# A linear-attention and feed-forward kernel: the hand-written TensorE order replaced, with later landings assumed for two kinds of transposing DMA

## The chip, the cores and the metric

The kernel runs on one core of a Trainium2 chip. The metric is the device time of one execution in microseconds (us); lower is better. The core has TensorE (PE in the profile, and PEld for its weight loads), VectorE (DVE), ScalarE (ACT), GpSimd (POOL) and SyncE (SP). SP does no arithmetic here. It issues nearly all DMAs, in the order of its own queue.

## The reference

```python
xn = layernorm(x)                          # x: 2048 x 448, bfloat16
q, k, v = split(xn @ wqkv)                 # 16 heads of 28
phi_q = concat(softmax(q @ w_phi), softmax(-(q @ w_phi)))   # per head, 28 + 28
phi_k = concat(softmax(k @ w_phi), softmax(-(k @ w_phi)))
kv = einsum("hsf,hsd->hfd", phi_k, v);  z = sum_s phi_k
o  = (phi_q @ kv) / (phi_q @ z + 1e-6)
out = x + o @ wo + silu(xn @ w1) @ w2      # w1: 448 x 1792, w2: 1792 x 448
```

## The kernel before

The 2048 tokens are 16 tiles of 128. The kernel records every operation with the buffers that it reads and writes, puts all of them in order with a list scheduler of its own (`schedule`), and emits one queue for each engine with the waits that the recorded dependences need. The scheduler's costs are figures written in the source. A DMA gets a time to issue, a transfer and a latency (`o.lat`).

For TensorE the order of most of the program is written out by hand, in the string `PLAN` (lines 334 to 342). Each word is one piece of work, and `strict` ties each TensorE operation to the one before it. The scheduler fits the other engines' queues to that order. The words are:

- `aF3@4`, `bF3`: first and second half of a feed-forward block, 256 columns of the hidden layer for 512 tokens, in PSUM banks 4 and 5. There are 28 blocks, seven for each 512 tokens. Blocks 0, 1 and 2 stand ahead of the plan. `av`, `ak` and `aq` with their `b` halves are the v, k and q projections of two tiles. The halves are matmuls on 64 rows of the array, two at a time: six in the first half, eight in the second. The second half waits until the first is finished (`o.after`).
- `f0@2`: one of four folds of w_phi into the q and k weights. Each takes two banks and needs all nine transposed weight loads `wT_dma0` to `wT_dma8`. ScalarE copies two reference columns out (`fold_ref`), and VectorE then takes them from the rest (`fold_sub`, line 636). Only after the third `fold_sub` of a fold are its banks free.
- `K0-6`: the sum over tokens phi_k x v for tiles 0 to 5. `M`: that sum is masked for use. `s4`: phi_q of tiles 4 and 5 is normalised on GpSimd and then transposed by a DMA named `phqT` (the first six in the order one tile at a time, the rest two at a time).
- `U4@2`: attention of tile 4 in bank 2. VectorE then divides by the denominator (`den`, `rden`, `o`), and a DMA named `oT_dma` transposes the result. `W4`: three matmuls with wo on that transposed tile. `R4,7`: the remaining rows of wo for tiles 4 and 7, as 64-row matmuls, and then the addition and the output's DMA. `F4@0:14` and `Y1:9`: the second feed-forward matmul, 14 or 9 of its 14 steps. `E15`: the end of the last tile, in two halves of 224 columns.

A word without `@` goes to the bank that the same tile or block already has. A `U` without one goes to bank 7.

The order of the DMAs on SP follows from the scheduler too. A `phqT` or `oT_dma` waits at the head of that queue until its data are there, and everything behind it waits as well. All `phqT` and `oT_dma` are issued by `dma_t` (line 583).

Of the kernel before, what the change touches and what calls it, by code (L numbers as in the profile page):

```python
# [8 lines left out]
ACTF = mybir.ActivationFunctionType  # L9
# [131 lines left out]
class _Prog:  # L141
# [76 lines left out]
    def schedule(self):  # L218
# [55 lines left out]
        while done < n:  # L274
# [56 lines left out]
TAIL = {"act": 110.0, "dve": 85.0, "pool": 45.0}  # L331
SIGNAL = {("act", "pe"): 60.0, ("act", "dve"): 40.0, ("dve", "pe"): 100.0, ("dve", "sp"): 30.0, ("dve", "dve"): 34.0,
          ("pool", "pe"): 100.0}
PLAN = """aF3@4 bF3 aF4@0 aF6@2 av2@6 bF4 bF6 aF5@4 av0@0 bv0 bF5 aF12@2 bv2 aF11@0 aF13@4 bF12 bF11 bF13 aF10@6 aF8@0 f0@2 f3@4
bF8 bF10 f2@2 aF9@0 f1@4 aF7@6 bF9 bF7 ak2@4 bk2 av12@6 av10@0 ak14@2 bv12 bk14 bv10 ak4@4 av14@6 bk4 ak0@2 bv14 av6@0
bk0 bv6 Y2@6:5 Y2:6 Y2:3 ak6@2 ak8@0 bk6 av8@4 av4@6 bv8 bk8 bv4 ak10@4 ak12@2 bk10 aq4@0 bk12 K0-2 bq4 aq6@4 K2-6 bq6
aq8@2 s4 aq0@0 bq8 K6-8 bq0 aF17@4 K8-10 bF17 aF14@2 aF19@0 bF14 bF19 aF16@4 aF23@2 K10-16 bF16 aF27@0 M bF23 bF27
aF24@5 aF20@2 bF24 aF26@0 bF20 aF15@4 bF26 s6 bF15 aF21@6 aF22@2 bF21 aF18@4 s8 bF22 s0 aF25@0 aq2@6 bF18 bF25 bq2
aq12@2 aq10@4 bq12 bq10 F9@1:2 F9:4 F9:8 U7 F7@6:10 s2 F7:4 Y1@5:2 Y0@0:6 U4@2 Y0:8 s10 U0@4 Y1:9 U9 Y1:3 F4@0:1 F4:13
U2 W4 U6@3 U3@5 W7 W9 s12 W0@2 R4,7 aq14@3 R0,9 bq14 Y3@5:2 Y3:3 U5@2 U1 F5@6:5 F5:9 U8@2 F6@0:11 F6:3 Y3:5 U13@2 U11  # L340
F11@4:14 Y3:2 U10@3 s14 W2@2 W5 W6 U12 F14@3:6 F10@1:7 U14 Y3:2 F10:7 F14:6 W10 F13@7:10 F14:2 W11 W14 R6,14 R5,10 R2,11
F13:4 F8@5:8 F8:4 F8:2 W3@6 W8 W13 F12@1:2 F12:1 F12:11 U15@0 W12 W1@4 R1,8,13 R12,3 F15@23:6 F15:8 E15"""


def bass_parallel_sum__linear_kernel_hedgehog__dense_activation_silu__prompt_kernel(
# [36 lines left out]
    with es:  # L382
        def sb(name, shape, dt):
            return es.enter_context(nc.sbuf_tensor(name, shape, dt))
# [46 lines left out]
        ones_bf = sb("ones_bf", [128, 128], BF16)  # L431
# [6 lines left out]
        warm_act = sb("warm_act", [128, 4], F32)  # L438
# [30 lines left out]
        def d_act(n):  # L469
            return n / 1.2 + 60.0  # L470
# [30 lines left out]
        def act(dst, src, func, n, name, scale=1.0, table=None, **keys):  # L501
            P.op("act", d_act(n), lambda e: e.activation(dst, src, func, scale=scale),  # L502
                 reads=[src], writes=[dst], table=table, name=name, **keys)
# [4 lines left out]
        def memset(dst, v, n, name, eng="pool"):  # L508
            P.op(eng, d_pool(n, 0.5), lambda e: e.memset(dst, v), writes=[dst], name=name)
# [12 lines left out]
        memset(epst[:], EPS_LN, 1, "epst")  # L522
        memset(neghalf[:], -0.5, 1, "neghalf")
        memset(ones4[:], 1.0, 4, "ones4")
        act(warm_act[:], ones_bf[:, 0:4], ACTF.Sqrt, 1460, "warm_act", table="sqrt")

        def block_mask(dst, w, n, m, off=0):
            tmp = mtmp[0:m, 0:n]
# [53 lines left out]
        def dma_t(dst, src, xfer, name, issue=1235.0, **kw):  # L582
            o = P.dma(lambda e: e.dma_start_transpose(out=dst, in_=src), xfer, lat=650.0, reads=[src] if kw.pop("sbuf", True) else [],  # L583
                      writes=[dst], name=name, issue=issue, **kw)
            o.crowd = 1
            o.lat += 700.0 if name in ("xnT_dma5", "xnT_dma7") else 0.0


        def fold():
# [12 lines left out]
        def fold_loads():  # L602
            for i in range(NW):
                c = max(0, KP * i - 64)
                dma_t(wT(i), A_wqkv[:, c:c + 128], 600.0, f"wT_dma{i}", 1800.0 if i == 2 else 1310.0, sbuf=False)
# [34 lines left out]
        def ln_tile(t):  # L640
# [21 lines left out]
            if t >= XN_DMA0:  # L662
                norm(xn_sb[:, sl, 0:KF], 0, KF, 370)
                norm(xn_sb[:, sl, KF:512], D - 128, D, 250)
                if t % 2:
                    dma_t(xnT[:, t - 1:t + 1, :, :].rearrange("p i k c -> p (i k) c"),
                          xn_sb[:, sl - 1:sl + 1, :].rearrange("p i c -> p (i c)"), 2200.0 if t < 8 else 1600.0, f"xnT_dma{t}", 1350.0)
                return
# [139 lines left out]
        def phi_q(t, pair=False):  # L808
            n = q_order.index(t)
            sp = n % NPQ  # L810
            Eq = eq(t)[:, 0, :].rearrange("p (c j f) -> p c j f", c=CC, f=DH)
            dst = phq[:, sp, :, 0:KP].rearrange("p c (j f) -> p c j f", f=DH)
            Rq = Rec[:, 0, t, :]
            P.op("pool", 1700, lambda e: e.tensor_tensor(dst, Eq, Rq.rearrange("p (c j) -> p c j", c=CC)[:, :, :, None].broadcast_to([128, CC, 4, DH]),  # L814
                                                         ALU.mult),
                 reads=[Eq, Rq], writes=[dst], name="phiq")
            if n % 2 or not pair:
                n0, sp0 = (slot(t) - 1, sp - 1) if pair else (slot(t), sp)
                w = slot(t) - n0 + 1
                dma_t(phT[:, n0:n0 + w, :, :].rearrange("p t c j -> p (t c) j"), phq[:, sp0:sp0 + w, :, :].rearrange("p n c j -> p (n c j)"),  # L820
                      (1900.0, 2500.0)[w - 1], "phqT", (1250.0, 2000.0)[w - 1])
# [11 lines left out]
        UB = 7  # L833
        yts = {int(w[1:].split(":")[0].split("@")[0]) for w in PLAN.split() if w[0] == "Y"}
        ob_cnt = [0]
# [159 lines left out]
        open_kind = {"F": F, "v": v_block, "k": k_block, "q": q_block}  # L995
        for word in PLAN.split():
            n0 = len(P.ops)
# [70 lines left out]
        for e in ("pe", "act", "dve", "pool"):  # L1068
            cnt = 0
            for oid in order[e]:  # L1070
                o = ops[oid]
# [4 lines left out]
        for e in ENGINES:  # L1076
            for oid in order[e]:
                o = ops[oid]
# [72 lines left out]
```

## Time and profile before

| | us |
|---|---|
| median of 4 runs | 149.83 |
| lowest and highest | 148.94 and 150.41 |
| the profiled execution: its own time | 150.41 |
| the profiled execution: its span | 149.1 |
| TensorE busy | 143.8 |
| VectorE busy | 91.2 |
| GpSimd busy | 74.2 |
| ScalarE busy | 71.8 |

Times in the profile are counted from the start of the span. The profiled execution is the slowest of the four runs. The granted TensorE clock was 1.0 throughout. TensorE's busy time by stage, from the profile's windows:

| stage | window us | length | TensorE busy |
|---|---|---|---|
| loads, layernorm, first blocks | 0 to 12.35 | 12.35 | 9.91 |
| feed-forward blocks and folds | 12.35 to 34.5 | 22.15 | 21.73 |
| k, v and q projections, sums K | 34.5 to 69.2 | 34.70 | 34.64 |
| feed-forward blocks | 69.2 to 90 | 20.80 | 20.80 |
| attention, second feed-forward matmul, output | 90 to 149.2 | 59.20 | 56.70 |

In a line of the timeline the columns are the start, the time from the first start to the last end of a merged run of instructions, the engine, the line, the operation with what it writes and reads, and how many; a bracket gives the idle time of the engine before it and what ended it.

### The profile page before, as it was taken

The page shows a single profiled execution, that of the slowest core. Times are in us where ns is not written, and L with a number is a line of the kernel's source. Part 1 is how long each engine was busy: PE and PEld are TensorE (multiplying, and loading weights), DVE is VectorE, ACT ScalarE, POOL GpSimd, SP SyncE. Part 2 cuts the span into 40 slices and gives each one's busy share as a digit, 9 for nine tenths or more (in the row PEclk, how much of TensorE's full clock was granted, in tenths as well). Part 3 has the DMA queues.
Part 4 walks back from the last instruction along what each step waited for, and adds up shares of the span by engine and source line. Part 5 has one row for each costly group of instructions (what it writes and reads, how often), then busy time and mean ns, then how long its engine had stood idle before and what let it go on. Part 6 is the DMA issues. An engine that isn't in the chain of part 4 may idle for free.

```text
span 149.1 us, 3741 instructions
## 1 busy us (share of the span) xinstructions
PE 143.8 (96%) x1572; PEld 79.9 (54%) x1572; DVE 91.2 (61%) x197; ACT 71.8 (48%) x92; POOL 74.2 (50%) x92
## 2 busy tenths in 40 slices
PE   7889999999999999999999999999999999999994
PEld 7775444554554557556444455555455555545563
DVE  2939898282699399506993006995779544226083
ACT  3646665669996599995756599200030000000000
POOL 8627567601089999996999700997000800000000
PEclk9999999999999999999999999999999999999999
DMA  4999964799920000000288390076799576305024
GB/s 105 333 357 236 271 131 73 144 144 272 338 77 2 0 0 4 4 0 4 42 157 157 70 145 0 0 150 79 137 201 208 120 133 126 70 4 185 0 66 156
DMA packets 44497, 17.54 MB, mean 118 GB/s; under 512 B 37040, under 2 KB 44096, under 8 KB 44480
## 3 DMA queue, kind: packets, MB, share of 16 engines
q1 hardware_dynamic: 41648, 15.10, 49.2%
q10 hardware_dynamic: 2704, 2.17, 4.8%
q8 instruction: 12, 0.20, 0.6%
q14 instruction: 5, 0.04, 0.1%
q0 software_dynamic: 128, 0.03, 0.1%
HBM read 6.57 MB, written 1.84 MB: 56 GB/s over the span
## 4 chain that ended last, share of the span: by engine, by line
PE 79%; DMA 8%; SPq 6%; DVE 5%; issue 1%; POOL 1%
PE psum L482 78%; SPq L583 5%; DMA phT<-in_B_w_dram 4%; DVE st L643 2%; DMA wT<-in_A_wqkv_dram 2%; DMA vaug<-vaug 2%; SPq L516 1%; DVE RA L658 1%; DVE mv L644 1%; DVE x_sb L896 1%; POOL rstd L654 0%; PE psum L497 0%; DVE xnT L506 0%; POOL ve L652 0%
## 5 line engine op out<-in xcount | busy, mean ns | idle before, releaser
L482 PE MATMUL psum<-xnT,phT 64*128 64x512 bf16 (+1 forms) x428 | 45.1, 350 | 1.5 <-DMA phT<-in_B_w_dram 0.7
L482 PE MATMUL psum<-w_sb,hT 128*128 128x448 bf16 (+1 forms) x238 | 45.1, 342 | 0.0
L778 DVE TENSOR_REDUCE Rec<-Ek_sb 128x32 f32<-128x896 bf16 (+1 forms) x20 | 24.4, 1252 | 24.6 <-ACT Ek_sb L502 17.9
L814 POOL TENSOR_TENSOR RA<-Ek_sb,Rec 128x896 bf16<-128x896 bf16 x16 | 27.0, 1721 | 22.1 <-issue 12.1
L482 PEld LDWEIGHTS psum<-xnT,phT 64*128 64x128 bf16 (+1 forms) x428 | 21.3, 95 | 21.4 <-DMA phT<-in_B_w_dram 0.9
L502 ACT ACTIVATE hT<-psum 128x1024 bf16<-128x1024 f32 x28 | 27.3, 1023 | 10.9 <-PE psum L482 10.9
L482 PEld LDWEIGHTS psum<-w_sb,hT 128*128 128x128 bf16 x238 | 22.2, 98 | 18.7 <-issue 1.5
L502 ACT ACTIVATE Ek_sb<-psum 128x864 bf16<-128x864 f32 x24 | 20.2, 916 | 19.5 <-DVE x_sb L896 16.0
L482 PE MATMUL psum<-Wqk,xnT 64*128 64x432 bf16 x224 | 23.3, 343 | 0.1
L788 POOL TENSOR_TENSOR Ek_sb<-Ek_sb,Rec 128x896 bf16<-128x896 bf16 x8 | 13.3, 1699 | 5.5 <-DVE Rec L779 5.5
L482 PEld LDWEIGHTS psum<-Wqk,xnT 64*128 64x128 bf16 x224 | 10.5, 95 | 10.1 <-issue 0.8
L788 POOL TENSOR_TENSOR phT<-phT,Rec 128x896 bf16<-128x896 bf16 x8 | 13.4, 1699 | 0.2 <-DVE Rec L779 0.2
L482 PE MATMUL psum<-wv,xnT 64*128 64x448 bf16 x112 | 12.6, 349 | 0.1
L896 DVE TENSOR_TENSOR x_sb<-psum,x_sb 128x448 bf16<-128x448 f32 (+1 forms) x13 | 7.1, 582 | 7.0 <-PE psum L482 7.0
L643 DVE BATCH_NORM_STATS2 st<-x_sb 128x6 f32<-128x448 bf16 x16 | 9.7, 603 | 2.8 <-DMA x_sb<-in_A_x_dram 2.8
L482 PE MATMUL psum<-wo_sb,vaug 128*128 128x448 bf16 (+1 forms) x51 | 10.7, 342 | 0.4 <-DMA vaug<-vaug 0.4
L874 DVE TENSOR_SCALAR den<-psum 128x16 f32<-128x16 f32 x16 | 2.4, 157 | 12.9 <-PE psum L482 12.9
L881 DVE TENSOR_TENSOR vaug<-psum,rden 128x448 bf16<-128x448 f32 x16 | 9.8, 623 | 0.4
L658 DVE TENSOR_SCALAR RA<-x_sb,mv,rstd 128x384 bf16<-128x384 bf16 (+4 forms) x29 | 8.9, 346 | 1.3 <-POOL rstd L654 1.1
L779 DVE RECIPROCAL Rec<-Rec 128x32 f32<-128x32 f32 (+1 forms) x24 | 8.7, 393 | 0.2
L482 PEld LDWEIGHTS psum<-wv,xnT 64*128 64x128 bf16 x112 | 5.4, 94 | 5.5 <-PE psum L482 0.5
L502 ACT ACTIVATE vaug<-psum 128x896 bf16<-128x896 f32 x8 | 7.4, 923 | 1.7 <-PE psum L482 1.7
(59 smaller groups left out, 113.0 us busy)
## 6 DMA issues: line engine op xcount, KB each, us to landing
out_dram<-x_sb ACTq DMA_DIRECT2D x15, 112.0 KB, 1.7
w_sb<-in_B_w_dram SPq DMA_DIRECT2D x1, 1568.0 KB, 8.2
x_sb<-in_A_x_dram SPq DMA_DIRECT2D x3, 448.0 KB, 7.0
wo_sb<-in_A_wo_dram SPq DMA_DIRECT2D x2, 336.0 KB, 7.2
phT<-in_B_w_dram SPq DMA_DIRECT2D x1, 576.0 KB, 7.9
phT<-in_B_w_dram SPq DMA_DIRECT2D x2, 256.0 KB, 5.2
phT<-in_B_w_dram ACTq DMA_DIRECT2D x1, 384.0 KB, 5.5
wv<-in_A_wqkv_dram SPq DMA_DIRECT2D x1, 336.0 KB, 7.9
```

The lines of the kernel that those rows point to most:

```text
L482: r = e.matmul(dst, lhsT, rhs, start=st, stop=sp, skip_group_check=True)
L502: P.op("act", d_act(n), lambda e: e.activation(dst, src, func, scale=scale), reads=[src], writes=[dst], table=table, name=name, **keys)
L583: o = P.dma(lambda e: e.dma_start_transpose(out=dst, in_=src), xfer, lat=650.0, reads=[src] if kw.pop("sbuf", True) else [], writes=[dst], ...
L643: P.op("dve", 590, lambda e: e.bn_stats(st6[:, t, :], xs), reads=[xs], writes=[st6[:, t, :]], name=f"bnst{t}", okeys_w=["ln"])
L658: P.op("dve", dur, lambda e: e.tensor_scalar(dst, x_sb[:, t, c0:c1], mv[:, t, 0:1], rstd[:, t:t + 1], ALU.subtract, ALU.mult), reads=[xs, ...
L778: P.op("dve", 50 + 967 * n, lambda e: e.tensor_reduce(R2, E4, AXL.X, ALU.add), reads=[E4], writes=[R2], name="Ssum")
L779: P.op("dve", 135 + 210 * n, lambda e: e.reciprocal(R2, R2), reads=[R2], writes=[R2], name="Rrec")
L788: P.op("pool", 1700, lambda e: e.tensor_tensor(E3, E3, Rk[:, :, None].broadcast_to([128, 32, DH]), ALU.mult), reads=[E3, Rk], writes=[E3], ...
L814: P.op("pool", 1700, lambda e: e.tensor_tensor(dst, Eq, Rq.rearrange("p (c j) -> p c j", c=CC)[:, :, :, None].broadcast_to([128, CC, 4, DH ...
L874: P.op("dve", 190, lambda e: e.tensor_scalar(den[:, uq, :], U3[:, :, DH], EPS_DEN, None, ALU.add), reads=[U3[:, :, DH]], writes=[den[:, uq ...
L881: P.op("dve", 620, lambda e: e.tensor_tensor(o3, U3[:, :, 0:DH], rden[:, uq, :, None].broadcast_to([128, H, DH]), ALU.mult), reads=[U3[:, ...
L896: P.op("dve", d_dve(cs.stop - cs.start), lambda e: e.tensor_tensor(res[:, cs], ob, addend[:, cs], ALU.add), reads=[ob, addend[:, cs]], wri ...
```

## The change

`PLAN` is another string. The same words of work appear in another order, with other banks, and with the second feed-forward matmuls cut at other places. Two figures of the scheduler are changed with it: the first activation on ScalarE (it stands for a table load) is taken to last longer, so that the second piece of w1, which ScalarE issues behind it, is reckoned with later, and each `oT_dma` and `phqT` is reckoned with 500 ns more latency. These figures are no instructions; only the order that the scheduler makes with them is.

```diff
-PLAN = """aF3@4 bF3 aF4@0 aF6@2 av2@6 bF4 bF6 aF5@4 av0@0 bv0 bF5 aF12@2 bv2 aF11@0 aF13@4 bF12 bF11 bF13 aF10@6 aF8@0 f0@2 f3@4
-bF8 bF10 f2@2 aF9@0 f1@4 aF7@6 bF9 bF7 ak2@4 bk2 av12@6 av10@0 ak14@2 bv12 bk14 bv10 ak4@4 av14@6 bk4 ak0@2 bv14 av6@0
...
-aq12@2 aq10@4 bq12 bq10 F9@1:2 F9:4 F9:8 U7 F7@6:10 s2 F7:4 Y1@5:2 Y0@0:6 U4@2 Y0:8 s10 U0@4 Y1:9 U9 Y1:3 F4@0:1 F4:13
-U2 W4 U6@3 U3@5 W7 W9 s12 W0@2 R4,7 aq14@3 R0,9 bq14 Y3@5:2 Y3:3 U5@2 U1 F5@6:5 F5:9 U8@2 F6@0:11 F6:3 Y3:5 U13@2 U11
...
-F13:4 F8@5:8 F8:4 F8:2 W3@6 W8 W13 F12@1:2 F12:1 F12:11 U15@0 W12 W1@4 R1,8,13 R12,3 F15@23:6 F15:8 E15"""
+PLAN = """aF3@4 bF3 aF5@0 aF4@2 av0@6 bF5 bF4 bv0 aF6@0 av2@4 bF6 bv2 aF13@6 aF11@2 bF13 aF12@4 bF11 aF10@6 bF12 bF10 aF8@0 f2@2
+f0@4 bF8 f3@6 aF7@2 aF9@0 f1@4 bF9 bF7 ak2@4 bk2 av12@6 av10@2 ak14@0 bv12 bk14 bv10 ak4@4 av14@6 bk4 ak0@0 bv14 ak6@2
+bk0 Y2@5:11 Y2:3 bk6 av6@6 ak8@0 bv6 bk8 av8@4 av4@2 ak10@6 bv4 bk10 bv8 ak12@2 aq4@0 bk12 K0-6 bq4 s4 aq8@2 aq6@4 bq8
+K6-8 aq0@0 bq6 bq0 aF14@2 K8-10 bF14 aF17@4 K10-12 aF19@0 bF17 bF19 aF23@2 K12-16 aF20@0 aF18@4 bF20 s6 s8 bF18 bF23
+aF15@0 aF27@4 M bF15 aF25@2 bF27 aF22@0 bF25 s0 aF21@4 aF16@6 bF21 bF22 bF16 aF24@4 aq2@2 aF26@0 bF24 bF26 aq10@6 bq2 s2
+bq10 U9@5 F4@4:14 F5@3:8 F5:6 U0@2 U7 aq14@0 aq12@5 bq14 bq12 s10 Y3@2:8 U5 F7@1:6 F7:6 F0@5:3 F0:2 F0:9 s12 Y3:6 F7:2
+U6@0 U4 W7 W0 F6@6:4 F6:3 W5 F9@0:4 F9:10 W9 F6:7 W6 U10 W4 R5,7 s14 R0,6 R9,4 F13@2:5 F12@1:7 F12:6 Y1@0:3 U15@4 U12@5
+Y1:11 U14 U13@6 F13:9 U8@0 F12:1 F10@3:5 U2@4 F8@6:9 F10:9 F8:2 U3@4 F11@0:3 W13 U1 F8:3 W8 F11:2 F11:9 U11 F14@5:14
+W1@4 W12 W14 R14,12 R1,8,13 W10 W3@7 W11 W2@1 F15@64:2 R10,11 R3,2 F15:6 F15:5 F15:1 E15"""
...
-        act(warm_act[:], ones_bf[:, 0:4], ACTF.Sqrt, 1460, "warm_act", table="sqrt")
+        act(warm_act[:], ones_bf[:, 0:4], ACTF.Sqrt, 2050, "warm_act", table="sqrt")
...
-            o.lat += 700.0 if name in ("xnT_dma5", "xnT_dma7") else 0.0
+            o.lat += {"xnT_dma5": 700.0, "xnT_dma7": 700.0, "oT_dma": 500.0, "phqT": 500.0}.get(name, 0.0)
```

In the built program TensorE has the same 1572 matmuls. The queues of SP, ScalarE and VectorE are the same up to the first halves of the plan; on GpSimd one small mask product (`bd0`, line 594) stands behind the first `ve` of the layernorm instead of ahead of it. In the later part SP's transposes, VectorE's divisions and ScalarE's evacuations follow the new TensorE order. There the two exponential steps of tiles 14 and 15 stand ahead of all outputs on ScalarE; before, they stood among the first outputs.

More of the change, by code (lines that the diff above doesn't have):

```diff
@@ L333 @@
           ("pool", "pe"): 100.0}
-PLAN = """aF3@4 bF3 aF4@0 aF6@2 av2@6 bF4 bF6 aF5@4 av0@0 bv0 bF5 aF12@2 bv2 aF11@0 aF13@4 bF12 bF11 bF13 aF10@6 aF8@0 f0@2 f3@4
-bF8 bF10 f2@2 aF9@0 f1@4 aF7@6 bF9 bF7 ak2@4 bk2 av12@6 av10@0 ak14@2 bv12 bk14 bv10 ak4@4 av14@6 bk4 ak0@2 bv14 av6@0
-bk0 bv6 Y2@6:5 Y2:6 Y2:3 ak6@2 ak8@0 bk6 av8@4 av4@6 bv8 bk8 bv4 ak10@4 ak12@2 bk10 aq4@0 bk12 K0-2 bq4 aq6@4 K2-6 bq6
-aq8@2 s4 aq0@0 bq8 K6-8 bq0 aF17@4 K8-10 bF17 aF14@2 aF19@0 bF14 bF19 aF16@4 aF23@2 K10-16 bF16 aF27@0 M bF23 bF27
-aF24@5 aF20@2 bF24 aF26@0 bF20 aF15@4 bF26 s6 bF15 aF21@6 aF22@2 bF21 aF18@4 s8 bF22 s0 aF25@0 aq2@6 bF18 bF25 bq2
-aq12@2 aq10@4 bq12 bq10 F9@1:2 F9:4 F9:8 U7 F7@6:10 s2 F7:4 Y1@5:2 Y0@0:6 U4@2 Y0:8 s10 U0@4 Y1:9 U9 Y1:3 F4@0:1 F4:13
-U2 W4 U6@3 U3@5 W7 W9 s12 W0@2 R4,7 aq14@3 R0,9 bq14 Y3@5:2 Y3:3 U5@2 U1 F5@6:5 F5:9 U8@2 F6@0:11 F6:3 Y3:5 U13@2 U11
-F11@4:14 Y3:2 U10@3 s14 W2@2 W5 W6 U12 F14@3:6 F10@1:7 U14 Y3:2 F10:7 F14:6 W10 F13@7:10 F14:2 W11 W14 R6,14 R5,10 R2,11
-F13:4 F8@5:8 F8:4 F8:2 W3@6 W8 W13 F12@1:2 F12:1 F12:11 U15@0 W12 W1@4 R1,8,13 R12,3 F15@23:6 F15:8 E15"""
+PLAN = """aF3@4 bF3 aF5@0 aF4@2 av0@6 bF5 bF4 bv0 aF6@0 av2@4 bF6 bv2 aF13@6 aF11@2 bF13 aF12@4 bF11 aF10@6 bF12 bF10 aF8@0 f2@2
[7 more added lines that the diff above has]
+W1@4 W12 W14 R14,12 R1,8,13 W10 W3@7 W11 W2@1 F15@64:2 R10,11 R3,2 F15:6 F15:5 F15:1 E15"""
 def bass_parallel_sum__linear_kernel_hedgehog__dense_activation_silu__prompt_kernel(
```

## The prediction

> **What bounds the kernel now.** I read the page's busy times first, then the chain of waits, then the timeline of TensorE at each place where the chain leaves it. The chain, in order of time (start, us, what):
>
> ```profile
> 25.25 3.04 DMA wT<-in_A_wqkv_dram
> 28.29 0.14 issue
> 28.43 2.58 PE psum L482 x62
> 31.01 0.03 issue
> 31.04 3.46 PE psum L482 x44
> 34.50 0.74 PE psum L482 x6
> 35.24 0.05 issue
> 35.29 68.84 PE psum L482 x856
> 104.12 2.49 DMA vaug<-vaug
> 106.61 0.05 issue
> 106.66 40.02 PE psum L482 x298
> 146.71 0.78 DVE x_sb L896 x2
> ```
>
> From 28.43 to 146.7 the end is set by TensorE alone, with one visit to a DMA. The reader is to see the 68.84 us without a break: no reordering can win there. Since the matmuls are the same 1572, the change can win only what TensorE loses between them. TensorE's timeline shows where:
>
> ```profile
> 28.43 0.39 PE L482 MATMUL psum<-BD,Y_sb 64*128 64x56 bf16 x16 [0.26 <-DMA wT<-in_A_wqkv_dram]
> ...
> 104.14 0.39 PE L482 MATMUL psum<-KVm,phT 112*128 112x58 bf16 x8
> 104.71 0.74 PE L482 MATMUL psum<-wo_sb,vaug 128*128 128x448 bf16 x3 [0.17 <-DMA vaug<-vaug]
> 105.28 0.62 PE L482 MATMUL psum<-KVm,phT 112*128 112x58 bf16 x16
> 105.75 0.73 PE L482 MATMUL psum<-wo_sb,vaug 128*128 128x448 bf16 x3
> 106.66 1.31 PE L482 MATMUL psum<-wo_sb,vaug 128*128 128x448 bf16 x6 [0.18 <-DMA vaug<-vaug]
> ```
>
> The brackets understate a loss, because a matmul's drawn end lies behind the time at which the next could start. So I go by starts. In undisturbed runs of the timeline a feed-forward matmul takes 0.108 us (22 from 16.62 to 19.00), so a first half takes 0.65, a second 0.86, a block 1.51. A v matmul takes 0.0945 (pair of halves 1.32), a k or q matmul 0.091, a wo or second feed-forward matmul 0.189, a U 0.23, a fold 0.21. By these TensorE loses, before:
>
> - 0.42 at the first fold. The 12 matmuls from 26.71 are through at 28.01, and it starts at 28.43, behind the last weight transpose, which lands at 28.29.
> - 0.27 at block 9 (31.04 instead of 30.77): block 8's activation in the same bank ends at 30.98.
> - 0.17 at the first k (34.50 instead of 34.33): the last `fold_sub` ends at 34.36.
> - 0.34 between U4 at 104.14 and W4 (104.71 instead of 104.37), and 0.34 before W7 (106.66 instead of 106.32). Both wait for an `oT_dma`; they land at 104.66 and 106.61.
> - 0.18 at tile 15: 143.43 instead of 143.25.
>
> Together 1.72 us.
>
> **The change, part by part.**
>
> *The two figures of the scheduler.* They issue nothing. Up to the first plan word every TensorE, ScalarE, VectorE and SP instruction stands as before: nothing, as long as GpSimd's moved mask product does nothing. It takes 0.26 and stands between `ve` (ends 11.95) and `rstd` of tile 4. This makes `rstd` of tiles 4 to 6 up to 0.25 late, but tile 7's waits for VectorE until 14.64 anyway, so the transposes behind it move by 0 to 0.1. I take 0.
>
> *Halves that follow each other.* A `b` directly behind its `a` waits for the first half to finish: the v pair from 19.00 takes 1.56, not 1.32. Before has three such places (blocks 3, v of tile 0, k of tile 2), after two: a gain of **0.23**.
>
> *Changes of array mode.* Between 64-row and full-array matmuls 0.10 is lost: six wo matmuls from 106.66 need 1.13, and the 64-row ones follow at 107.90. After changes mode 12 times instead of 10: a loss of **0.19**.
>
> *The folds.* Block 3 starts at 13.01. Ahead of the first fold now stand eight whole blocks, two v blocks, a first half and one followed pair: 8 x 1.51 + 2 x 1.32 + 0.65 + 0.23, so the fold is reached at 28.61 (before, at 28.01, with block 10's second half behind it). That is 0.32 behind the transpose's landing: **0.42 is gone**. What is late next are the fold's own banks, since block 7 goes to bank 2 after one second half and two folds: 28.61 + 3 x 0.21 + 0.86 = 30.11. The rows for a fold's evacuation, from VectorE's and ScalarE's timelines:
>
> ```profile
> 29.14 0.73 DVE L636 TENSOR_TENSOR Wqk<-psum,last_lo 128x54 bf16<-128x54 f32 x2 [2.82 <-ACT last_hi L502]
> 29.79 0.54 DVE L636 TENSOR_TENSOR Wqk<-psum,last_hi 128x378 bf16<-128x378 f32 x1
> ```
>
> ```profile
> 26.11 1.94 ACT L502 ACTIVATE hT<-psum 128x1024 bf16<-128x1024 f32 x2
> 28.85 0.19 ACT L502 ACTIVATE last_lo<-psum 128x18 f32<-128x18 f32 x1 [0.81 <-PE psum L482]
> ```
>
> Reference at 28.85, third subtraction done at 30.33: 1.48 later. After, ScalarE first has the activations of blocks 12 and 10. Block 12 ends at 27.10, ScalarE starts 0.21 later (as at 33.47 to 33.68), the pair takes 1.94: until 29.25. The references overlap it by 0.09, so they start at 29.16, the third subtraction ends at 30.64, and TensorE follows 0.14 later, as at 34.36 to 34.50. Block 7 starts at 30.78, **0.67 late**. No row of before shows this wait: 0 if VectorE gets through sooner, and 1.77 if all six subtractions of both folds (done at 31.74) had to pass. I take 0.67, since banks are released fold by fold before. Then block 9 (31.43) finds block 8's activation done (31.13): **0.27 is gone**. The last fold is at 32.08, its references at 32.51, and VectorE, busy with the third fold until 32.83, ends at 33.99; the first k comes at 34.13 instead of 34.02: **0.11** in place of 0.17. So the first k starts 0.37 earlier than before.
>
> *Projections, sums and blocks (34 to 88).* I laid out each queue by its rows. GpSimd's 16 phi_k products at 1.66 start at 41.15 and end at 67.75; K12-16 is reached at 68.64. ScalarE's nearest calls are block 20 (reached 0.1 after its bank is free) and q of tile 8 (0.3). Before has such places and loses nothing in its 68.84 us. I take 0, with 0 and 0.3 as ends.
>
> *Attention (88 to 149).* W4 and W7 are moved far from their U, so **0.68 is gone**. SP's queue after: `phqT` of tiles 2 and 3 from 96.4 (when GpSimd's second product ends), `oT` of U0 and U7, `phqT` of 10 and 11 from 100.9 to 102.9, `oT` of U5 at 104.05 (VectorE divides it only behind the row sums of tiles 12 to 15), `phqT` of 12 and 13 from 106.3 to 108.2, `oT` of U6 and of U4 to 110.8. The durations:
>
> ```profile
> L583 SPq DMA_TRANSPOSE vaug<-vaug x15: 1188/1267/2249, 99.3 to 127.7; - x15
> ...
> DMA to landing us min/median/max: 2.4/3.1/4.2
> ```
>
> TensorE reaches W5 at 108.1, W6 at 113.2, W4 at 114.0. With the median of 3.1 from issue to landing the three have landed at 107.2, 111.4 and 112.6. With the slowest, 4.2, W5 is 0.15 late and W4 0.3 early; a `phqT` issue of 2.85, as at 111.94, brings W4 to 0.6 late. I take 0, with 0 and 0.75 as ends. From 115 on each transposed tile has 2 us or more to spare.
>
> [...]
>
> *The end.* The first two steps of tile 15 now come before R10,11 and R3,2, whose time covers the wait for bank 6: **0.18 is gone**. Bank 6 is free at 141.64 and wanted at 141.81. The rest of the end is the same work.
>
> Sum: -1.72 - 0.23 + 0.19 + 0.67 + 0.11 = **-0.98 us**. The profiled execution took 150.41 (span 149.1), so its like would take 149.43; against the median of 149.83, which is 0.58 below that execution, I forecast **148.85**.
>
> **The rivals.**
>
> 1. *The fold's banks are free in time.* For: the 0.67 rests on ScalarE having two activations ahead of the references. Against: the rows add up with nothing left open. 148.85 - 0.67 = 148.2.
> 2. *W5 and W4 still meet their transposes*, by the slow issues and landings that before shows. For: two `phqT` of two tiles now stand ahead of them. Against: the room of 0.9 and 1.4 at the median. 148.85 + 0.75 = 149.6.
> 3. *Losses only change place.* The order rests on reckoned durations, which did not foresee 1.72 us before, and several calls have 0.1 to 0.3 to spare. As much comes back as goes: 149.8.
> 4. *Slower: SP's queue clogs between 106 and 114.* `phqT` of tiles 12 and 13 stands ahead of the `oT` of U6 and U4. With all three at the longest issues (2.85, 2.25, 2.25) the last is issued at 113.7 and lands up to 2.9 later, at 116.6, so W4 stalls 2.6: 151.45. It costs nothing up to a landing at 114.0, and decides (over 1% slower) from 116.5. Against: of 15 only two took about 2 us or more to issue.
>
> **How the numbers follow.** Forecast 0.42, rival 1 0.15, rival 2 0.18, rival 3 0.13, rival 4 0.12. A measurement of this kernel can tell about 1% from no change: below 148.33 or above 151.33. Faster: rival 1 and 0.08 of the forecast (its 0.5 us to the bound is within the spread of 148.94 to 150.41 between like runs), 0.23. Slower: 0.13, rival 4 and a trace of rival 3. Within 1%: 0.64. The range goes from 148.0 (rival 1, less 0.2) to 150.3 (rival 3, and 0.5 of spread); rival 4 is left out.
>
> **What would show it.** The first fold without a wait for the weight transpose, and the first block on the fold's bank 0.67 late, waiting for VectorE; k from about 34.1; no wait for a transposed tile behind 100; the end of TensorE one us earlier. A wait for `vaug` between 107 and 115 would show rival 2 or 4; waits for ScalarE between 36 and 90, rival 3. I am wrong most easily in what I could not see before: the transposes' landings in a queue of another order.

## The result and the profile after

| | before | after |
|---|---|---|
| median, us | 149.68 (71 runs, 148.94 to 151.86) | 149.23 (45 runs, 148.71 to 152.67) |
| the profiled execution: its own time, us | 150.41 | 149.67 |
| the profiled execution: its span, us | 149.14 | 147.89 |
| own time minus span, us | 1.27 | 1.78 |

The ratio is 0.9973, with a 95% interval of 0.9964 to 0.9983; it leaves out slow executions, such as the one of 152.67. The changed kernel is 0.3% faster, some 0.45 us by the medians; 0.98 were forecast (148.85). The last row of the table is where the rest went. The span of the profiled execution shrank by 1.25, but what lies outside the span grew by 0.51.

The page of the changed kernel opens with the span and the busy times:

```profile
span 147.9 us, 3735 instructions
...
PE 143.0 (97%) x1572; PEld 79.8 (54%) x1572; DVE 91.0 (61%) x196; ACT 71.6 (48%) x92; POOL 74.0 (50%) x92
```

The chain of waits of the changed kernel, from the second half of the first planned block on (start, length, what):

```profile
13.62 13.42 PE psum L482 x126
27.04 0.02 issue
27.06 1.94 ACT hT L502 x2
29.00 0.08 ACT last_lo L502
...
29.32 1.06 DVE Wqk L636 x2
30.38 0.05 issue
30.42 4.11 PE psum L482 x49
34.53 0.04 issue
34.58 110.85 PE psum L482 x1184
145.43 0.02 issue
145.45 0.78 DVE x_sb L896 x2
```

Both DMAs that the prediction shows in the chain of before are gone: the weight transpose at 25.25 and the transposed tile at 104.12. From 34.58 TensorE runs 110.85 us without a break; before, it ran 68.84 and 40.02 with a wait between. One visit to other engines is new. The chain goes through two activations of ScalarE (27.06), its reference columns (29.00) and VectorE's subtractions (29.32), and returns to TensorE at 30.42. TensorE's timeline shows which step waits there:

```profile
28.36 0.39 PE L482 MATMUL psum<-BD,Y_sb 64*128 64x56 bf16 x16
...
30.42 1.47 PE L482 MATMUL psum<-xnT,phT 64*128 64x512 bf16 x12 [0.34 <-DVE Wqk L636]
...
33.79 1.69 PE L482 MATMUL psum<-Wqk,xnT 64*128 64x432 bf16 x14
```

The first fold starts at 28.36 with no bracket. Block 7, in the bank of the first fold, starts at 30.42 and waits for VectorE. By the undisturbed steps of the prediction it loses 0.58, where 0.67 was forecast. The first k, at 33.79, loses 0.10, where 0.11 was forecast. These are the only two places behind the first planned block where TensorE waits for another engine.

In the attention stage the wo matmuls stand without brackets:

```profile
104.92 0.62 PE L482 MATMUL psum<-KVm,phT 112*128 112x58 bf16 x16
105.38 1.30 PE L482 MATMUL psum<-wo_sb,vaug 128*128 128x448 bf16 x6
...
107.84 0.73 PE L482 MATMUL psum<-wo_sb,vaug 128*128 128x448 bf16 x3
...
113.75 0.73 PE L482 MATMUL psum<-wo_sb,vaug 128*128 128x448 bf16 x3
```

The matmuls at 107.84 are W5, those at 113.75 W4. SP's queue, which brings their tiles:

```profile
101.43 2.09 SPq L583 DMA_TRANSPOSE phT<-RA  x1
103.85 1.30 SPq L583 DMA_TRANSPOSE vaug<-vaug  x1
107.27 1.75 SPq L583 DMA_TRANSPOSE phT<-RA  x1
109.07 3.17 SPq L583 DMA_TRANSPOSE vaug<-vaug  x2
112.33 1.86 SPq L583 DMA_TRANSPOSE phT<-RA  x1
```

The tile of U5 is issued at 103.85 and lands at 106.41, 1.43 us before W5. The tile of U4 is the second of the two from 109.07 on: it is issued at 110.97 and lands at 113.53, only 0.22 us before W4.

### The profile page after: what moved, and what is told of

Read it like the earlier page. It is cut to its first block, busy times and chain, and to the rows that moved or that the text cites. A ratio compares the mean times of both kernels' runs of the same rounds, so it can differ in the third digit from the quotient of the medians.

```text
span 147.9 us, 3735 instructions
## 1 busy us (share of the span) xinstructions
PE 143.0 (97%) x1572; PEld 79.8 (54%) x1572; DVE 91.0 (61%) x196; ACT 71.6 (48%) x92; POOL 74.0 (50%) x92
## 4 chain that ended last, share of the span: by engine, by line
PE 90%; DMA 4%; ACT 2%; DVE 1%; SPq 1%; issue 0%
PE psum L482 90%; DMA phT<-in_B_w_dram 4%; ACT hT L502 1%; SPq L516 1%; DVE Wqk L636 1%; DVE x_sb L896 1%; PE psum L497 0%; ACT last_hi L502 0%; ACT last_lo L502 0%
## 5 line engine op out<-in xcount | busy, mean ns | idle before, releaser
L482 PE MATMUL psum<-xnT,phT 64*128 64x512 bf16 (+1 forms) x428 | 45.6, 350 | 1.6 <-DMA phT<-in_B_w_dram 1.0
L778 DVE TENSOR_REDUCE Rec<-phT 128x64 f32<-128x1792 bf16 x4 | 8.0, 2006 | 0.6 <-ACT phT L502 0.6
```

Of the source, the lines that this page charges most:

```text
L482: r = e.matmul(dst, lhsT, rhs, start=st, stop=sp, skip_group_check=True)
L778: P.op("dve", 50 + 967 * n, lambda e: e.tensor_reduce(R2, E4, AXL.X, ALU.add), reads=[E4], writes=[R2], name="Ssum")
```

## The experiments

Kernels sent to the chip together ran on one chip and share the runs of the kernel before. A table gives medians of the runs: the span, what the time holds beyond the span, and the time. TensorE's losses are read from the profiled execution of each kernel, as in the prediction: actual starts against undisturbed steps. The diffs show the words of the plan that change, with line breaks set anew; `...` stands for the rest.

### The change again, and its two halves

*again* is the changed kernel, unaltered. *head_only* is the kernel before with the first words of the plan, up to the first k, taken from the changed one. The scheduler's figures are those of before.

```diff
-aF3@4 bF3 aF4@0 aF6@2 av2@6 bF4 bF6 aF5@4 av0@0 bv0 bF5 aF12@2 bv2 aF11@0 aF13@4 bF12 bF11 bF13 aF10@6 aF8@0 f0@2 f3@4
-bF8 bF10 f2@2 aF9@0 f1@4 aF7@6 bF9 bF7
+aF3@4 bF3 aF5@0 aF4@2 av0@6 bF5 bF4 bv0 aF6@0 av2@4 bF6 bv2 aF13@6 aF11@2 bF13 aF12@4 bF11 aF10@6 bF12 bF10 aF8@0 f2@2
+f0@4 bF8 f3@6 aF7@2 aF9@0 f1@4 bF9 bF7
 ak2@4 bk2 av12@6 av10@0 ak14@2 bv12 bk14 bv10 ak4@4 av14@6 bk4 ak0@2 bv14 av6@0
...
```

*rest_only* is the other half: the words of before up to the first k, and all else of the changed kernel, its two figures included. *w_late* is the kernel before with nothing but W4 and W9 moved behind other steps:

```diff
...
-U2 W4 U6@3 U3@5 W7 W9 s12 W0@2 R4,7
+U2 U6@3 U3@5 W7 W4 s12 W0@2 W9 R4,7
...
```

What was expected of each:

> The changed kernel once more, beside the kernel before on the same chip. Theory A (the sum read from one execution holds in every execution): 0.98 us less than before, a ratio of 0.9935, and a profile like the first one: the first block on the fold's bank waits 0.6 us for VectorE, TensorE waits nowhere behind 40 us. Theory B (part of the 1.72 us that TensorE lost in the profiled execution of before was that execution's own late DMA landings, and typical executions lose less): 0.4 to 0.5 us less, a ratio near 0.997, with the same profile. Theory C (the changed kernel has its own late landings in other executions): a profile with a wait for a transposed tile or for the weight transposes of 0.3 us or more.

> The new order up to the first k projection, the old order from there on. Theory A: k starts 0.37 us earlier and nothing else changes, so 0.37 us less, a ratio of 0.9975; the two waits for a transposed tile between 104 and 107 stay. Theory B, with the wait for the weight transpose as the chance part: before reaches the fold at 28.0 in any execution and loses only what the landing is late, so with a landing at 27.7 instead of 28.29 the gain is 0 to 0.1 us, a ratio of 0.999 to 1.000. Theory B with the transposed tiles alone as the chance part: 0.37 us less, as by A.

> The old order up to the first k projection, the new order and the scheduler's new figures from there on. Theory A: the two waits for transposed tiles (0.68) and the 0.18 at tile 15 go, two more changes of array mode cost 0.19: 0.67 us less, a ratio of 0.9955. Theory B with the transposed tiles as the chance part: 0 to 0.3 us less, 0.998 to 1.000. Theory B with the weight transpose as the chance part: 0.67 us less.

> The kernel before with only the order of seven plan words changed (U2 U6 U3 W7 W4 W0 W9 instead of U2 W4 U6 U3 W7 W9 W0), so that W4 comes 1.0 us and W9 0.6 us later after their transposes; the work is the same. Theory A: the 0.34 us ahead of W4 goes whole and of the 0.34 us ahead of W9 some 0.25: 0.55 to 0.6 us less, a ratio of 0.996. Theory B with the transposed tiles as the chance part: 0 to 0.2 us less, a ratio of 0.9985 to 1.000.

Measured:

| | span | time minus span | time | ratio to before, 95% |
|---|---|---|---|---|
| before | 149.00 | 1.28 | 150.24 | 1 |
| again | 147.85 | 1.81 | 149.63 | 0.9973 (0.9954 to 0.9993) |
| head_only | 148.25 | 1.29 | 149.55 | 0.9958 (0.9932 to 0.9985) |
| rest_only | 148.35 | 1.79 | 150.15 | 0.9998 (0.9975 to 1.002) |
| w_late | 148.30 | 1.28 | 149.57 | 0.9966 (0.994 to 0.9992) |

Three things follow. First, the span of the change falls by 1.15 on one chip, a little more than the forecast 0.98. The time falls by 0.61 only, because 0.53 is paid outside the span. Second, those 0.53 come with the second half: rest_only pays them, head_only and w_late don't. In rest_only, 0.51 of this kind eat most of the gain in the span, which is 0.65; the time doesn't differ from that of before (0.9975 to 1.002), where 0.9955 was expected. Third, moving two words gains about as much in the time (0.67) as the whole new order does. The gains of the two halves in the span, 0.75 and 0.65, add up to 1.40, 0.25 more than the whole shows; that is within the intervals of the ratios, which are 0.3 to 0.4 us to each side.

The rival that the profiled execution of before had met unusually late landings falls. The wait for a transposed tile stands in head_only as before; its chain of waits:

```profile
103.95 2.49 DMA vaug<-vaug
106.48 40.02 PE psum L482 x298
146.53 0.78 DVE x_sb L896 x2
```

Again 2.49 us of a landing stand between two stretches of TensorE, and TensorE loses 0.44 there and 0.26 ahead of W4. With the two words moved, TensorE's timeline of w_late has the twelve wo matmuls in one piece, without a bracket:

```profile
103.83 0.84 PE L482 MATMUL psum<-KVm,phT 112*128 112x58 bf16 x24
104.52 2.52 PE L482 MATMUL psum<-wo_sb,vaug 128*128 128x448 bf16 x12
106.97 0.36 PE L482 MATMUL psum<-wor_sb,vaug 64*128 64x448 bf16 x2
```

The wait for the weight transpose is another matter. In rest_only, with the head of before, the first fold waits longer than in before itself (chain of waits):

```profile
25.05 3.01 DMA wT<-in_A_wqkv_dram
28.06 0.14 issue
28.20 2.58 PE psum L482 x62
...
35.06 110.85 PE psum L482 x1184
```

It loses 0.91 here against 0.42 in before, for the first planned block started at 12.28 and not at 13.01, while the transpose lands where it did (28.06 and 28.29). The changed head meets this wait too when it starts early: again loses 0.49 there, head_only 1.05. The wait is a race between the start of the blocks and a landing, and its size is different in each execution.

### What lies outside the span

The half microsecond had to be in something that comes with the second half of the new plan and not with the first. SP's queue is one such thing: the built program has 80 instructions on SP in before, head_only and w_late, and 79 in the changed kernel and rest_only, one wait on a semaphore fewer. SP's queue ends with the waits for the outputs:

```python
if ename == "sp":
    for i in range(NOS):
        if out_cnt[i] > 0:
            eng.wait_ge(out_sems[i], 16 * out_cnt[i])
```

Two of these waits make one instruction: with four semaphores the traces of before and of the changed kernel have two instructions of this line (1119) at the end of SP's queue. With another number of output semaphores (`NOS`, line 451) SP's code gets longer or shorter, and TensorE's order stays as it is. *sp80* and *sp81* are the changed kernel with 5 and 8:

```diff
-        NOS = 4
+        NOS = 8
```

*before_sp79* is the kernel before with 2. *act130* is the changed kernel with waits that are long met put ahead of the first output on ScalarE. It makes ScalarE's code one instruction longer and leaves SP's at 79:

```diff
+                if ename == "act" and o.name == "out_dma" and not waited.get("pad"):
+                    waited["pad"] = 1
+                    for other in ("pool", "dve", "pe"):
+                        eng.wait_ge(eng_sem[other], 1)
```

> The changed kernel with five semaphores for the outputs' DMAs instead of four: SP gets one more instruction at its end (80 instead of 79, as many as before the change), and nothing else moves. So far the time of an execution less its span is 1.2 to 1.3 us with 80 instructions on SP (before, head_only, w_late) and 1.7 to 1.8 with 79 (the changed kernel, rest_only). Theory D (the missing 0.5 us of the gain lies behind the span: SP's code ends at a place where the next instruction has to be fetched): time less span 1.25 to 1.35, span 147.8 as in the changed kernel, so 1.0 to 1.1 us less than before, a ratio of 0.993. Theory E (something else of the new order's second part lies behind the span: GpSimd's and VectorE's shorter or ScalarE's longer code): time less span stays at 1.75 or more, ratio 0.997.

> The changed kernel with eight such semaphores: SP has 81 instructions. Theory D, with 79 as the one bad place: time less span 1.25 to 1.4. Theory D', each further instruction on SP costs at the end, or only an even number is good: 1.75 or more. Theory E: 1.75 or more.

> The kernel before with two such semaphores instead of four: SP has 79 instructions. Theory D: time less span 1.75, the span as before (149.0), so 0.45 to 0.5 us more than before, a ratio of 1.003. Theory E: time less span 1.2 to 1.3, ratio 1.000.

> The changed kernel with one more, already satisfied wait on ScalarE ahead of the first output's DMA (130 instructions there, 79 on SP). Theory D: time less span stays at 1.75 to 1.85. If ScalarE's code length were the cause, it would change by about 0.5.

Measured (one run each of sp81 and act130):

| | instructions on SP | span | time minus span | time | ratio to before, 95% |
|---|---|---|---|---|---|
| before | 80 | 148.50 | 1.26 | 149.75 | 1 |
| before_sp79 | 79 | 148.50 | 1.81 | 150.31 | 1.0042 (1.0026 to 1.0059) |
| act130 | 79 | 147.5 | 1.76 | 149.26 | |
| sp80 | 80 | 148.00 | 1.29 | 149.34 | 0.9974 (0.9959 to 0.999) |
| sp81 | 81 | 147.4 | 1.30 | 148.70 | |

The kernel before gets the half microsecond as well once its SP code has 79 instructions, with TensorE's order as it was: same span, 0.55 more time. One instruction more on ScalarE changes nothing (act130: 1.76 outside the span, where the changed kernel has 1.78 to 1.81). With 81 instructions on SP the changed kernel loses the half microsecond. The number of semaphores isn't what decides: with four of them head_only has 1.29 outside the span and rest_only 1.79.

sp80 is the instructive miss. Its time minus span fell to 1.29 as expected, but its span is 0.6 us longer than in the one run of sp81, and its ratio to before (0.9974, where 0.993 was expected) is no better than that of the changed kernel. TensorE is not the cause: its last matmul starts at 144.98 in sp80 and at 145.11 in sp81, but from there to the end of the span pass 2.85 in sp80 and 2.34 in sp81. The trace of SP's last instructions tells what happens. Times are us from the end of the span, which in all kernels is the end of SP's last wait:

```
                79th instruction   80th instruction            81st          last output   first semaphore
                of SP ends         of SP begins                begins        has landed    update behind the span
before          -1.13              -0.41 (output at -0.43)     -             -0.02         +0.14
after            0.00              -                           -             -0.02         +0.66
before_sp79      0.00              -                           -             -0.02         +0.66
sp80            -0.49              -0.03 (outputs by -0.51)    -             -0.51         +0.18
sp81            -1.05              -0.59 (outputs by -1.47)    -0.41         -0.02         +0.13
folds_early     -1.05              -0.57 (outputs by -1.49)    -0.41         -0.02         +0.13
```

In brackets stands when the outputs that the 80th instruction waits for had landed. In sp80 all outputs have landed at -0.51 and the 79th instruction is through at -0.49, yet the 80th begins only at -0.03: 0.46 us in which SP waits for nothing. In sp81 the same gap, 0.46 us, stands between the same two instructions, while the last output is still on its way. In before it has room between -1.13 and the landing at -0.43. In the changed kernel the 79th instruction is the last of the program, so that a gap behind it falls behind the end of the span: the first update of a semaphore comes 0.52 later there than in before. The gap itself is seen only where an 80th instruction has nothing to wait for: in sp80, sp81, sp81_again and folds_early. That the other kernels have it too is inferred from the fit. What it costs then depends on what stands beside it: nothing where an output is awaited anyway (before, sp81), half a microsecond in the span (sp80) or behind it (after, before_sp79, act130).

### The better version, and an attempt at the folds

*sp81_again* is the kernel with eight output semaphores once more, *after_same_chip* the changed kernel beside it. *folds_early* is sp81 with the folds placed otherwise, so that block 7 doesn't need the bank of a fold. The v of tile 6 moves with it, from behind the first k's to either side of the first half of the first k:

```diff
...
-aF8@0 f2@2 f0@4 bF8 f3@6 aF7@2 aF9@0 f1@4 bF9 bF7 ak2@4 bk2 av12@6 av10@2 ak14@0 bv12
+aF8@0 f2@2 f0@4 bF8 aF7@6 f3@2 bF7 aF9@0 f1@4 bF9 av6@2 ak2@4 bv6 bk2 av12@6 av10@0 ak14@2 bv12
...
-av6@6 ak8@0 bv6 bk8 av8@4 av4@2 ak10@6
+ak8@0 av8@4 bk8 av4@2 ak10@6
...
```

> The changed kernel with eight output semaphores in place of four, which makes SP's code 81 instructions long (79 in the changed kernel); the order of TensorE is that of the changed kernel. Theory D (the missing half microsecond lies behind the span, because SP's code ends where it does): own time minus span 1.3, own time about 148.5 to 148.8, ratio to the kernel before 0.9925 to 0.994, and 0.5 us below the changed kernel on the same chip. Without D: the same ratio as the changed kernel, 0.997.

> The changed kernel itself on the same chip as the run above, to compare the two directly. Theory D: own time minus span 1.75 to 1.85, ratio 0.997, 0.5 us above the run with the longer SP code, with spans that agree within 0.2. Without D: no difference between the two.

> The changed kernel with eight output semaphores and the places of the folds altered: block 7 goes to bank 6 before the third fold and the third fold into bank 2 behind it, so that no block has to wait until a fold's bank is read; the first half of v of tile 6 stands ahead of the first k. If the 0.58 us at block 7's bank is a loss of its own, block 7 starts without a wait for VectorE, the first k waits 0.1 to 0.4 for the last fold, which is now reached later by the order, and the whole gains 0.2 to 0.5 on the run with the longer SP code alone: ratio 0.990 to 0.992. If the loss only moves to the next that waits for the folds (the first k late by 0.6 or more), the two take the same time within 0.1.

Measured:

| | span | time minus span | time | ratio to before, 95% |
|---|---|---|---|---|
| before | 148.40 | 1.28 | 149.73 | 1 |
| after_same_chip | 147.40 | 1.79 | 149.19 | 0.9964 (0.9941 to 0.9986) |
| sp81_again | 147.35 | 1.25 | 148.62 | 0.993 (0.9913 to 0.9947) |
| folds_early | 148.45 | 1.25 | 149.71 | 0.9996 (0.9985 to 1.0008) |

The spans of the changed kernel and of sp81_again agree within 0.05, and the times are 0.57 apart. That is the version that beats both kernels: the new order with SP's code two instructions longer, 1.1 us less than before, about what the forecast gave the order alone.

folds_early lost 1.1 us on sp81_again where 0.2 to 0.5 were to be gained. Block 7's wait is gone, as meant, but four others came. TensorE's timeline of folds_early:

```profile
29.94 0.36 PE L482 MATMUL psum<-BD,Y_sb 64*128 64x56 bf16 x15
...
33.77 0.72 PE L482 MATMUL psum<-Wqk,xnT 64*128 64x432 bf16 x6 [0.26 <-DVE Wqk L636]
...
42.48 0.72 PE L482 MATMUL psum<-Wqk,xnT 64*128 64x432 bf16 x6 [0.72 <-ACT vaug L502]
...
49.62 0.55 PE L482 MATMUL psum<-wv,xnT 64*128 64x448 bf16 x4 [0.25 <-DVE Y_sb L852]
```

By starts the third fold (29.94) loses 0.17, the first k 0.42, the k at 42.48 loses 0.91 and the v at 49.62 0.42. The first two are the folds' loss in another place: the third fold, now in the first fold's bank, waits for that fold's last subtraction (done at 29.79), and the first k for the last fold's (33.62). Together they cost 0.59, as much as block 7's bank and the first k in sp81_again, 0.58. The other two, 1.33, are new. The halves of the k pair of tile 2 no longer follow each other, which saves the 0.25 that this pair loses in sp81_again; 1.1 is left, as measured. The chain of waits of folds_early leads to the largest of the four:

```profile
39.10 0.92 ACT vaug L502
40.02 1.59 ACT phT L502 x2
41.62 0.81 ACT vaug L502
42.43 0.05 issue
42.48 2.77 PE psum L482 x28
```

ScalarE evacuates the v and k banks in the order in which TensorE fills them. The v of tile 6, put ahead of the first k as a filler, put its own evacuation (0.92, at 35.29) ahead of ScalarE's table load for the exponentials (`ACT_TABLE_LOAD`, 1.28). That load began at 36.23, and at 34.30 in sp81_again. All later evacuations followed late (the first exponentials at 37.52 and not at 35.59, the v bank behind them at 39.10 and not at 37.27), and the bank of the v of tile 10 came free at 42.43. So the loss at the folds only moved, even with half a v as a filler ahead of the first k, and 1.33 were lost further down, the larger part of it behind that filler's evacuation. An order without the loss was not found; another filler was not tried.

## Why the prediction was right and where it was wrong

**The waits that were to go.** The two waits for transposed tiles, the 0.27 of block 9 and the 0.18 at tile 15 are gone in every execution of the new order. They were no chance of one execution: with before's plan, head_only and before_sp79 show them again (0.26 and 0.29 ahead of W4, 0.44 and 0.41 at the second place, 0.18 at tile 15; block 9's 0.27 in before_sp79, which has before's head). The prediction named the second place W7; by the order of `PLAN` the matmuls that wait at 106.66 are W9's, and the tile is that of U9. The U at 104.14, just ahead of W4, is U2 and not U4. From the first k to the end the span holds 114.64 in before and 114.10 in the changed kernel, and 114.09 to 114.10 in six more executions of the same order whose span doesn't hold the gap of sp80: a gain of 0.54. The forecast left 0.61 for this part (0.98 less the 0.37 up to the first k).

**The first fold.** "0.42 is gone" holds in the profiled execution of the changed kernel, in sp80 and in sp81, not in general. The prediction placed the fold at 28.61 by starting block 3 at 13.01, as before did. In the changed kernel it started at 12.74, in the other executions between 11.74 and 12.42, and in five of those with the new head the fold waits again: 0.49 in again, 1.05 in head_only, 0.24 in after_same_chip, 0.29 in act130, 0.40 in sp81_again. That it didn't in the first profile was partly luck. The sum suffers little, for before's head meets more of the same (0.69 in w_late, 0.91 in rest_only, 0.28 in before_sp79). On the chip of sp80 and sp81 the first k started at 33.70 with before's head and at 33.23, 33.36 and 33.39 with the new one: 0.37 earlier, which is what the prediction gave. These are single executions, though, and block 3 started 0.14 earlier in the three than in the one, so the close agreement is chance.

**The fold's banks.** The 0.67 is there, at the step and behind the engine that were named, and measures 0.58, or 0.48 where the fold itself came late. The 0.11 at the first k measures 0.10. Rival 1 fails.

**SP's queue.** Rivals 2 and 4 fail, but not by the room that the forecast saw. W4 was to find its tile 1.4 us early at the median landing. It found it 0.22 early in the profiled execution, and between 0.18 and 0.40 early in eight others. The landing itself was quick, 2.56 from issue; the issue was late, 110.97 to 112.24, some 1.5 later than reckoned. The phi_q transpose of two tiles ahead of it was through at 109.02, 0.8 later than reckoned, and the issue of U6's tile behind that took 1.85 instead of 1.3. A delay of another 0.22 in the issues would have brought the wait back.

**Behind the issue.** The time from the end of an issue to the landing is not one figure: U4's tile landed 2.88 us behind the end of its issue in before and 1.29 behind it in the changed kernel. The waits stood again in head_only and before_sp79, which keep the order of before there.

**The step that failed** is the one that turned the span into the time: "The profiled execution took 150.41 (span 149.1), so its like would take 149.43". The sum of -0.98 was one of TensorE's losses within the span, and there it holds: the medians give -1.15 on one chip and -1.00 on another. The step took the 1.27 us outside the span as fixed. They became 1.78, since the new order leaves SP one wait instruction fewer. That the number of SP's instructions decides is shown by before_sp79, sp81 and sp81_again; that it is the gap behind the 79th, which then falls behind the program's end, is inferred from SP's last instructions. With the 0.51 put in, the forecast for the measured pair is 149.68 - 0.98 + 0.51 = 149.21; 149.23 was measured. The prediction laid out SP's transposes one by one and counted none of its instructions. That the count went from 80 to 79 stood in the two built programs; that it had a price could not be read from the trace of before, where the gap has an awaited landing to hide it.

**Losses only change place**, rival 3 (149.8), fails by its own mechanism: no new wait for ScalarE stands between 36 and 90 in the changed kernel. Rival 2's 149.6 is as near to the measured time as the forecast, without the wait that would have made it. The place that the gain went to is not on TensorE, and no rival named it.

## What to carry to other kernels

Keep two sums: what an edit does within the span, and what the time holds outside it. Compare time minus span across kernels before any loss is looked for in the span, since a constant difference of a few tenths there (0.51 to 0.55 here) is a cause of its own. Where the final waits of an engine stand at the program's end, let the wait for the latest landing be the last and others precede it, so that a gap in that engine's own issue lies beside a transfer (the 0.46 us cost nothing in sp81 and lengthened the span in sp80); and before a step is put in as a filler, look at what evacuates it and what then comes late behind that evacuation (in folds_early the bank of the v of tile 10 held TensorE up by 0.91 us).

## What had not been expected of the hardware

- SP loses 0.46 to 0.47 us between its 79th and 80th instruction in sp80, sp81, sp81_again and folds_early, with nothing to wait for; the 79th follows the 78th, a wait as well, after 0.04 us in the same kernels.
- One transfer of 8192 bytes on the queue that the page lists as "q14 instruction" starts between -0.04 and +0.60 us from the span's end in the kernels with 80 or 81 SP instructions, and between +1.10 and +1.28 in those with 79. Counted from the end of SP's 79th instruction it starts 1.09 to 1.28 us later in all thirteen profiles, so it goes with that place in SP's code. But in sp80 the 80th instruction began 0.63 us before this transfer, so the gap is no wait for it. What SP does in the gap stays open: theory D of sp80 supposed the fetch of an instruction, and the runs settle only the place in SP's code and the 0.46 us, not the cause.
- The start of the first planned block differs by 1.3 us between executions of the same head (11.74 to 13.01 over thirteen of them, whose operations up to there are the same but for one small mask product).
